# Gated MLP kernel: weight pieces of the second half with raw loads two ahead, at other points of a batch, U and V as one piece

## The chip, the cores and the metric

The kernel runs on one core of a Trainium2 chip. Its time is the device time of one execution in microseconds (us); the median of several executions is compared. The engines are TensorE (PE, with its weight load PEld), VectorE (DVE), ScalarE (ACT) and GpSimd (POOL); SyncE (SP) issues nearly all DMAs. Each engine works through its own instructions in the order in which they are written, and waits for others by semaphores.

## The reference

Three stages follow each other: a linear attention over 8 batches and 8 heads, a gated MLP with a mix over the tokens, and a mix over channels with a low-rank part. Cut to what matters:

```python
# stage 1: attention, 8 batches, 8 heads, 576 tokens, head size 64 -> x (8, 576, 512)
# stage 2
h = np.maximum(x @ w_in, 0.0)                  # w_in 512 x 1024
u, v = h[..., :512], h[..., 512:]
v_n = (v - mean(v)) / sqrt(var(v) + 1e-06)      # over the last axis
v_s = einsum('ts,bsd->btd', w_spatial, v_n) + b_spatial[None, :, None]
x = (u * v_s) @ w_out                          # w_out 512 x 512
# stage 3
u = x + (x.transpose(0, 2, 1) @ U @ V).transpose(0, 2, 1)   # U 576 x 32, V 32 x 576
out = u + np.maximum(u @ w_ch1, 0.0) @ w_ch2   # w_ch1 512 x 2048, w_ch2 2048 x 512
```

The inputs q, k, v and the spatial weights are float32; w_in, w_out, U, V, w_ch1 and w_ch2 arrive as float64, and the kernel turns them into float32 itself.

## The kernel before

A float64 weight comes as pairs of 32-bit words. `fetch_weight` (L35) issues the load of a piece into a tile "raw" (L53) and returns the repack: ACT makes `low` from the low words (L62), DVE makes `bits` in three operations (L67, L71, L75), ACT squares the high words for the size (L80), and a last DVE operation (L87) writes the float32 piece. A full piece is 128 x 512 (512 KB raw). The tiles `low`, `bits` and the stage tile "w32" (`stage`, L170), into which most pieces are written, exist once each; raw loads alternate between "raw" and "raw2" (`raws`, L174). A piece of w_ch1, and half of w_ch2, is written from the stage tile to DRAM (tensors w1d and w2r, 256 KB a piece). Four pairs of w_ch2 rows are repacked into the tile `w2`, POOL makes sums of their blocks in `z2` (`left_sums`), and both are split into a float32r high and low part (`w2s`) and stored (w2d). For the left factors, blocks of w1d are read back and handled likewise (`left`).

Matrix products use such splits: of x = hi + lo three products are summed (hi hi, hi lo, lo hi; `products`, L773). PSUM pool "a" has four banks, which all outputs of the gated stage take in turn, so the tile four places later waits until an output has been read.

The attention runs first, to about 371 us of the span, with its own weight steps for w_in, w_spatial and w_out. Then come eight batches of the gated stage, some 64 us each, and from about 886 us the channel stage. A batch's tokens lie in four tiles of 128 and one of 64. A batch is, in PE's order:

- `gate`: eight outputs pu (four f, two column halves; 12 matmuls of 128 x 288 each), whose relu on ACT (L908) gives u; then eight outputs pz (14 matmuls each) of the normalised values with the spatial weights, which DVE multiplies with u (L929); ACT and POOL (or DVE for the last f) split the result into g.
- `gated_open`, `gated_out`: px, g times w_out, for five token tiles; ACT copies it (L961), DVE splits it (xh, xl).
- `low_rank`: pr, and `low_rank_out` its split t1; `mixed`: transposes pt and py, added on DVE and stored.
- Between these, `values` of the next batch: pv, relu on ACT (L840), for the last tile an addition on DVE (L843) and a maximum (L844); statistics on DVE (L849 to L851), a power on POOL (L852), the normalising (L857) and casts on DVE and the difference on POOL. `normalize` of a tile is called in `values` of the next one, ahead of its statistics.

Weight steps lie between: `work()` (L874) is called four times in the pu loop, twice in the pz loop and twice around the first half of `mixed`. One call does the next step of the piece at hand and, where that ends, issues the load of the piece behind it: so one raw load is under way at a time. Which pieces a batch has is fixed: batch 0 U, V and two of w_ch1, batches 1 to 4 three pieces and a pair of w_ch2 rows each, batch 5 the rest, batches 6 and 7 left factors. A scheduler orders instructions on each engine by the written order and by `issue_after(self.last[...])`, which holds a step's instructions behind the last relu and the last DVE operation noted. ACT sets the whole of `ua` and `ub` to zero with nine copies (L285, L287) before U's parts are written there.

## Time and profile before

| | |
|---|---|
| runs, median (lowest to highest) | 1631.65 us (1629.53 to 1633.07), 3 runs |
| profiled execution, its own time | 1628.22 us |
| its span | 1626.4 us |
| PE busy | 1563.1 us, 96% of the span |
| DVE, ACT, POOL busy | 1170.4, 883.0, 807.8 us (72%, 54%, 50%) |
| mean granted clock of PE | 0.995 |
| attention / gated stage / channel stage | 0 to 371 / 371 to 886 / 886 to 1626 us |

The rows below come from this one execution. A window row gives for a stretch how long each engine was busy, so its length less PE's busy time is PE's idle time there; PEclk is the share of the full clock that PE was granted. A timeline row gives start, length, engine, line and operation, output and inputs, how many instructions were merged, and in brackets the idle time in front of it and the instruction that ended it. In a row of line groups the last part is the idle time before all of them, with what ended most of it.

### The profile page before, as it was taken

What the parts mean: (1) busy time and instruction counts of PE and PEld (TensorE: products, weight loads), DVE (VectorE), ACT (ScalarE), POOL (GpSimd) and SP (SyncE); (2) the same over time, 40 slices, a digit from 0 to 9 for tenths busy, and PEclk for the clock granted to TensorE, in tenths of its full rate; (3) what the DMA queues carried; (4) which work ended last, traced back from release to release, by engine and by line L of the source; (5) the groups of instructions that cost most, each with busy time, mean ns of one, the idle gap of its engine ahead of it and who ended that gap; (6) DMA issues with size and microseconds to landing.
All of it is one profiled execution on the core that took longest, in us unless ns stands there. A gap on an engine that the chain in (4) does not pass through costs nothing.

```text
span 1626.4 us, 30538 instructions
## 1 busy us (share of the span) xinstructions
PE 1563.1 (96%) x11592; PEld 1462.6 (90%) x11592; DVE 1170.4 (72%) x1642; ACT 883.0 (54%) x1668; POOL 807.8 (50%) x610
## 2 busy tenths in 40 slices
PE   7999999998999999999999999999999999999998
PEld 7998889887888888797978899999999999999998
DVE  6888767865766766766565578788877777777765
ACT  5888768883443443443434555555555555555443
POOL 3678777674342443442434256546554455444442
PEclk9999999999999999999999999999999999999999
DMA  4677766652342442533427678999899877777876
GB/s 139 188 204 205 213 189 189 198 146 71 102 136 92 142 130 88 171 98 105 160 96 313 225 242 281 305 315 316 293 343 396 268 231 234 239 248 237 259 242 233
DMA packets 172182, 336.72 MB, mean 207 GB/s; under 512 B 25794, under 2 KB 96610, under 8 KB 168964
## 3 DMA queue, kind: packets, MB, share of 16 engines
q1 hardware_dynamic: 171892, 334.72, 64.1%
q8 instruction: 91, 1.49, 0.4%
q14 instruction: 55, 0.45, 0.1%
q10 hardware_dynamic: 144, 0.07, 0.0%
HBM read 251.58 MB, written 73.55 MB: 200 GB/s over the span
## 4 chain that ended last, share of the span: by engine, by line
PE 69%; DVE 12%; DMA 8%; ACT 5%; issue 3%; POOL 2%; SPq 1%; DVEq 0%; ACTq 0%; POOLq 0%
PE pc L779 19%; PE ph_x L779 11%; PE ph_z L779 6%; PE pv L779 5%; PE pn L616 5%; PE pkv L588 4%; PE pu L779 4%; PE ph_y L779 3%; PE pk L515 2%; PE pt L547 2%; DMA raw_c<-in_w_ch 2%; DMA w1d<-w_c 1%; PE pq L515 1%; PE pt L997 1%; DVE bits_c L67 1%
## 5 line engine op out<-in xcount | busy, mean ns | idle before, releaser
L779 PE MATMUL pc<-hc,w 128*128 128x288 f32 x2688 | 420.3, 295 | 3.2 <-ACT hc L146 1.2
L779 PEld LDWEIGHTS pc<-hc,w 128*128 128x128 f32 x2688 | 378.1, 188 | 4.2 <-ACT hc L146 2.9
L779 PE MATMUL ph_x<-us,cw 128*128 128x288 f32 x1536 | 244.9, 295 | 3.3 <-DVE us L149 3.3
L569 POOL TENSOR_TENSOR qp<-e,qp 128x576 fp32r<-128x576 f32 x128 | 183.9, 1459 | 115.9 <-ACT e L566 87.9
L779 PEld LDWEIGHTS ph_x<-us,cw 128*128 128x128 f32 x1536 | 217.2, 188 | 4.3 <-DVE us L149 3.7
L616 PE MATMUL pn<-qp,kv 128*65 128x288 f32 x768 | 206.0, 328 | 8.8 <-DVE nd L625 4.2
L1096 POOL TENSOR_TENSOR t<-h,h 128x576 f32<-128x576 f32 x64 | 113.4, 1773 | 183.0 <-DVE hc L149 164.7
L149 DVE TENSOR_TENSOR hc<-t,hc 128x576 fp32r<-128x576 f32 x128 | 132.2, 1035 | 50.2 <-ACT hc L146 49.9
L1155 ACT COPY u<-ph_x 128x288 f32<-128x288 f32 x128 | 51.2, 400 | 191.0 <-PE ph_x L779 190.9
L588 PE MATMUL pkv<-v,kp 128*128 128x65 f32 x1024 | 153.1, 252 | 0.0
L588 PEld LDWEIGHTS pkv<-v,kp 128*128 128x128 f32 x1024 | 151.7, 191 | 0.0
L779 PE MATMUL ph_z<-us,cw 128*128 128x288 f32 x768 | 124.5, 297 | 8.7 <-DVE c L1160 8.5
L149 DVE TENSOR_TENSOR hc<-h,hc 128x576 fp32r<-128x576 f32 x96 | 125.0, 1305 | 9.6 <-ACT hc L146 9.5
L779 PEld LDWEIGHTS ph_z<-us,cw 128*128 128x128 f32 x768 | 107.9, 188 | 13.4 <-DVE c L1160 13.1
L1096 POOL TENSOR_TENSOR t<-u 128x576 f32<-128x576 f32 x32 | 48.9, 1528 | 137.6 <-DVE us L149 120.4
L1096 POOL TENSOR_TENSOR t<-h,t 128x576 f32<-128x576 f32 x64 | 111.8, 1748 | 9.0 <-DVE hc L149 6.5
L779 PE MATMUL pz<-wt,vn 128*128 128x288 f32 x768 | 112.5, 295 | 2.3 <-DVE u L929 2.2
L1168 ACT ACTIVATE h<-c 128x288 f32<-128x288 f32 x192 | 85.3, 445 | 54.2 <-DVE c L1160 53.9
L616 PEld LDWEIGHTS pn<-qp,kv 128*65 128x65 f32 x768 | 97.8, 138 | 14.6 <-DVE nd L625 5.4
L779 PE MATMUL pu<-xs,wi 128*128 128x288 f32 x768 | 104.9, 298 | 4.4 <-DVE v L843 4.4
L779 PEld LDWEIGHTS pu<-xs,wi 128*128 128x128 f32 x768 | 104.2, 190 | 5.4 <-DVE v L843 4.6
L779 PEld LDWEIGHTS pz<-wt,vn 128*128 128x128 f32 x768 | 105.2, 188 | 3.1 <-DVE u L929 3.1
(169 smaller groups left out, 3153.3 us busy)
## 6 DMA issues: line engine op xcount, KB each, us to landing
w<-w2d SPq DMA_DIRECT2D x224, 512.0 KB, 4.9
u<-ud SPq DMA_DIRECT2D x16, 1152.0 KB, 5.4
raw_c<-in_w_ch SPq DMA_DIRECT2D x32, 512.0 KB, 4.2
cw<-w1x SPq DMA_DIRECT2D x8, 1792.0 KB, 10.0
v<-in_v SPq DMA_DIRECT2D x32, 325.0 KB, 4.2
k<-in_kT SPq DMA_DIRECT2D x32, 320.0 KB, 3.4
q<-in_qT SPq DMA_DIRECT2D x32, 320.0 KB, 4.0
x<-nd SPq DMA_DIRECT2D x64, 144.0 KB, 3.3
```

The lines of the kernel that those rows point to most:

```text
L67: nc.vector.tensor_scalar(out=bits, in0=hi, scalar1=3, scalar2=0x3FFFFFF8, op0=ALU.logical_shift_left, op1=ALU.bitwise_and,)
L149: return self.put((nc.gpsimd if elo == "pool" else nc.vector).tensor_tensor(out=lo, in0=src, in1=hi, op=ALU.subtract))
L515: self.pin(nc.tensor.matmul(pa[:, j * NF + t, :], x[d, t * P : (t + 1) * P], ws[d, :], start=True, stop=True,))
L547: self.pin(nc.tensor.transpose(pt[:, at, :], s[:, u, :], self.ident))
L569: self.pin(nc.gpsimd.tensor_tensor(out=lo[:, c], in0=e[:, c], in1=hi[:, c], op=ALU.subtract))
L588: self.pin(nc.tensor.matmul(pkv[:, i, j, :], kp[:, j * NF + t, :], vb[:, u * D1 : (u + 1) * D1], start=False, stop=(j == 1 and t == NF - 1),))
L616: self.pin(nc.tensor.matmul(pn, kv[k][:, i, g // 2, :], qp[q][:, i, g * HS : (g + 1) * HS], start=(m == 0), stop=(m == len(terms) - 1),))
L779: self.put(self.nc.tensor.matmul(out, x, y, start=(start and i == 0), stop=(stop and i == len(terms) - 1), skip_group_check=chained,))
L997: nc.tensor.transpose(pt[:, s0 - c0 : s0 - c0 + n], ts[t][0][:n, fs], self.ident[:n, :n])
L1096: self.put(self.nc.gpsimd.tensor_tensor(out=out, in0=p, in1=q, op=ALU.subtract))
L1155: self.put(nc.scalar.copy(out, src))
L1168: self.put(nc.scalar.activation(self.h[n, t // 2, x][:, t % 2], src, AF.Relu))
```

## The change

The late weights (U, V, w_ch1, w_ch2 and the left factors) become one list of 49 units, made once by `units()`. `prefetch()` issues the raw loads of the next two raw units, alternately into "raw" and "raw2"; `work()` does one unit and then prefetches. Each raw unit is a full piece: conversion, last operation and store in one step. U (two copies of its last rows) and V (in two column halves, each held twice) are one piece of 128 x 448 with seven loads and one repack; only the places of `ua` and `ub` that hold no U are zeroed, from a tile of zeros set at the start.

`work()` is now called four times in the pu loop, not in the pz loop, and then once after the px tiles are begun, once behind `low_rank_out` and once in the middle of `mixed`: seven units a batch for batches 0 to 6, none in batch 7. Batches 1 to 3 have store pieces throughout but for the last units of batch 3; pairs, their parts and left factors fill batches 4 to 6. The stage tile, `low` and `bits` still exist once. `low_rank_out` notes its two last instructions in `last`. The pad of `vn` is written behind the values of batch 0 (`pad()`), and a tile's statistics and power are written ahead of the normalising of the tile before it. The order of PE's instructions is the same. New line numbers: L67, L71, L75, L87 become L111, L115, L118, L121; L62 and L80 become L110 and L120; L908 becomes L937; L929 becomes L958.

```diff
+    def fetch(self, parts, name):
+        nc, raw = self.nc, None
+        if any(src.dtype != F32 for _, src in parts):
+            tag, pool = (("raw", self.sp), ("raw2", self.mq))[self.fetched % 2]
+            self.fetched += 1
+            raw = pool.tile([P, 2 * PIECE], I32, tag=tag, name=f"{tag}_{name}", bufs=1)
+            for view, src in parts:
+                nc.sync.dma_start(view(raw, 2), src.bitcast(I32))
+
+        def into(dst):
+            if raw is not None:
+                return repack_doubles(nc, self.sp, dst, raw, name)
...
+        def low_rank():
...
+            into = self.fetch(parts, "uv")
+
+            def step():
+                a = self.stage("uv", c1 + HS)
+                into(a)
...
+                nc.scalar.copy(ub[:, :, 2 * R : 3 * R], z)
+                nc.scalar.copy(ua[tail:, NF, 2 * R : 3 * R], z[tail:, 0])
+                for i in (0, 1, 3):
+                    nc.scalar.copy(ua[:, :, i * R : (i + 1) * R], w)
+                    nc.scalar.copy(ub[:, :, i * R : (i + 1) * R], w[:, :NF])
...
+                for h in range(2):
+                    r, c = slice(h * R, (h + 1) * R), slice(h * HS, (h + 1) * HS)
+                    for i in range(3):
+                        nc.scalar.copy(vs[i * R : (i + 1) * R, c], v[r])
...
         def piece(dst, src, name):
             def load():
+                into = self.fetch([(whole, src)], name)
+
+                def step():
+                    w = self.stage(name, PIECE)
+                    into(w)
                     nc.sync.dma_start(dst, w)
+                return step
             return load
...
+    def prefetch(self):
+        raws = 0
+        for i, u in enumerate(self.todo):
+            kind, f, step = u
...
+            if kind == "raw":
+                raws += 1
+                if raws > 2:
+                    break
+                if step is None:
+                    u[2] = f()
+
+    def work(self):
+        if not self.todo:
+            return
+        kind, f, step = self.todo.pop(0)
+        with self.tc.issue_after(self.last[0]), self.tc.issue_after(self.last[1]):
+            (step if kind else f)()
+        self.prefetch()
...
@@ values
-        self.normalize()
         st = mq.tile([P, 6], F32, tag="st", name=f"st{b}_{t}", bufs=2)
...
         nc.gpsimd.tensor_tensor(
             out=rstd[:n], in0=rstd[:n], in1=self.mhalf[:n, :1], op=ALU.pow
         )
+        self.normalize()
@@ gate
-            if f < self.KH - 2:
-                self.work()
@@ low_rank_out
-        nc.scalar.copy(t1, pr)
+        act = nc.scalar.copy(t1, pr)
...
+        self.last[:2] = act.ins, dve.ins
@@ main loop
+    mx.units()
+    mx.prefetch()
     for t in range(NST):
         mx.values(0, t)
+    mx.pad()
...
         begun = [mx.gated_open(b, t) for t in range(3)]
+        mx.work()
```

DVE in the gate of batch 2, before, where pu ends and pz begins (`bits_c`, `w_c` and `w` belong to weight pieces, `u_0` and `u_1` are multiplied with pz):

```order
L67 TENSOR_SCALAR bits_c_3_512_6231<-raw_c_3_512_6198 128x512
L71 SCALAR_TENSOR_TENSOR bits_c_3_512_6231<-raw_c_3_512_6198,bits_c_3_512_6231 128x512
L929 TENSOR_TENSOR u_0_6082<-pz_0_0_6242,u_0_6082 128x288
L75 ISA bits_c_3_512_6231<-bits_c_3_512_6231,low_c_3_512_6229 128x1024
L929 TENSOR_TENSOR u_0_6082<-pz_0_1_6260,u_0_6082 128x288
L87 SCALAR_TENSOR_TENSOR w_c_3_512_6197<-low_c_3_512_6229,bits_c_3_512_6231 128x512
L67 TENSOR_SCALAR bits_c_1_0_6282<-raw_c_1_0_6239 128x512
L71 SCALAR_TENSOR_TENSOR bits_c_1_0_6282<-raw_c_1_0_6239,bits_c_1_0_6282 128x512
L929 TENSOR_TENSOR u_1_6118<-pz_1_0_6288,u_1_6118 128x288
L75 ISA bits_c_1_0_6282<-bits_c_1_0_6282,low_c_1_0_6280 128x1024
L929 TENSOR_TENSOR u_1_6118<-pz_1_1_6306,u_1_6118 128x288
```


and after:

```order
L111 TENSOR_SCALAR bits_c_3_1536_6223<-raw_c_3_1536_6149 128x512
L115 SCALAR_TENSOR_TENSOR bits_c_3_1536_6223<-raw_c_3_1536_6149,bits_c_3_1536_6223 128x512
L118 ISA bits_c_3_1536_6223<-bits_c_3_1536_6223,low_c_3_1536_6222 128x1024
L958 TENSOR_TENSOR u_0_6106<-pz_0_0_6275,u_0_6106 128x288
L121 SCALAR_TENSOR_TENSOR w_c_3_1536_6221<-low_c_3_1536_6222,bits_c_3_1536_6223 128x512
L111 TENSOR_SCALAR bits_c_4_6264<-raw_c_4_6190 128x512
L115 SCALAR_TENSOR_TENSOR bits_c_4_6264<-raw_c_4_6190,bits_c_4_6264 128x512
L958 TENSOR_TENSOR u_0_6106<-pz_0_1_6293,u_0_6106 128x288
L118 ISA bits_c_4_6264<-bits_c_4_6264,low_c_4_6263 128x1024
L958 TENSOR_TENSOR u_1_6151<-pz_1_0_6311,u_1_6151 128x288
L121 SCALAR_TENSOR_TENSOR w_c_4_6262<-low_c_4_6263,bits_c_4_6264 128x512
L958 TENSOR_TENSOR u_1_6151<-pz_1_1_6329,u_1_6151 128x288
```


The first multiplication by u_0 stood ahead of two operations of the third piece and stands now ahead of the last one alone; the second has moved from ahead of that piece's last operation (L87, now L121) to behind it and behind two operations of a fourth store piece. The second multiplication by u_1 stood ahead of a last operation into `w2` and stands now behind one into the stage tile.

ACT in the gate of batch 0, before (L908 is the relu of pu; `low_u` is a part of U being repacked, `ub` a copy of U):

```order
L908 ACTIVATE u_1_4777<-pu_1_1_4792 128x288
L62 ACTIVATE low_u_4806<-raw_u_4775 128x128
L80 ACTIVATE low_u_4806<-raw_u_4775 128x128
L908 ACTIVATE u_2_4818<-pu_2_0_4819 128x288
L908 ACTIVATE u_2_4818<-pu_2_1_4833 128x288
L62 ACTIVATE low_u_4847<-raw_u_4814 64x32
```


and after (L937 is the relu):

```order
L120 ACTIVATE low_uv<-raw_uv 128x448
L937 ACTIVATE u_1_4804<-pu_1_1_4819 128x288
L353 CAST ua<-w_uv 128x5x32
L354 CAST ub<-w_uv 128x4x32
L353 CAST ua<-w_uv 128x5x32
L354 CAST ub<-w_uv 128x4x32
L353 CAST ua<-w_uv 128x5x32
L354 CAST ub<-w_uv 128x4x32
L362 CAST vs<-w_uv 32x288 x6
L110 ACTIVATE low_c_0_0_4834<-raw_c_0_0_4611 128x512
L937 ACTIVATE u_2_4845<-pu_2_0_4846 128x288
```


The relu of the third u, first half, stood behind one small piece of U; it stands now behind the whole of U and V, six copies to `ua` and `ub`, six to `vs`, and the first conversion of a piece of w_ch1.

DVE at the first values tile of batch 0, before (`w_pad` is the pad, `st_0`, `mv_0` and `rstd_0` the statistics):

```order
L849 BN_STATS st_0_4624<-v_0_4607 128x6
L648 RECIPROCAL den_31_4569<-den_31_4569 128x9
L765 MEMSET w_pad 64x512
L850 BN_AGGR mv_0_4625<-st_0_4624 128x2
L767 MEMSET w_pad 1x512 x2
L851 TENSOR_SCALAR rstd_0_4626<-mv_0_4625 128x1
L768 CAST vn_4600<-w_pad 64x512
L857 TENSOR_SCALAR v_0_4607<-v_0_4607,mv_0_4625,rstd_0_4626 128x512
```


and after:

```order
L807 MEMSET w_pad 64x512
L809 MEMSET w_pad 1x512 x2
L640 TENSOR_TENSOR kv_31_4471<-pkv_4391,kv_31_4470 128x260
L663 TENSOR_SCALAR nd_4483<-pn_1_4492,eps 65x288
L686 RECIPROCAL den_29_4465<-den_29_4465 128x9
L663 TENSOR_SCALAR nd_4533<-pn_1_4542,eps 65x288
L686 RECIPROCAL den_30_4526<-den_30_4526 128x9
L810 CAST vn_4602<-w_pad 64x512
L890 BN_STATS st_0_4631<-v_0_4614 128x6
L686 RECIPROCAL den_31_4571<-den_31_4571 128x9
L891 BN_AGGR mv_0_4632<-st_0_4631 128x2
L892 TENSOR_SCALAR rstd_0_4633<-mv_0_4632 128x1
```


The pad's memsets stood among the statistics of the first tile; they stand now in front of the last attention operations, and the cast of the pad ahead of the first statistics.

## Rows read from the trace of the kernel before

**Rows 1.** Windows by batch: from:to length, busy us PE, PEld, DVE, ACT, POOL; PEclk.

```profile
370.96:434.29 63.33, 56.70 (x329) 50.99 (x328) 40.46 (x84) 27.32 (x69) 25.46 (x23) 0.97 0.32 99
434.29:497.70 63.41, 61.05 (x359) 53.04 (x358) 43.92 (x81) 27.35 (x56) 23.80 (x24) 1.00 0.38 121
497.70:559.97 62.27, 60.61 (x359) 53.20 (x358) 45.38 (x82) 27.41 (x56) 24.81 (x24) 1.00 0.40 123
559.97:623.67 63.70, 61.23 (x358) 53.04 (x358) 43.63 (x82) 27.39 (x56) 23.81 (x24) 1.00 0.39 120
623.67:688.28 64.61, 61.13 (x359) 53.11 (x358) 47.39 (x82) 27.31 (x56) 28.48 (x28) 1.00 0.41 127
688.28:755.19 66.91, 63.62 (x358) 54.91 (x358) 44.42 (x85) 27.26 (x56) 20.48 (x20) 0.95 0.34 99
755.19:820.25 65.06, 61.30 (x359) 53.16 (x358) 43.28 (x76) 27.04 (x55) 29.37 (x28) 1.00 0.43 141
820.25:886.50 66.25, 65.55 (x384) 57.58 (x384) 38.32 (x74) 25.42 (x51) 24.22 (x24) 0.98 0.55 214
```

**Rows 2.** Windows, as rows 1, of four short stretches with PE stalls.

```profile
393.00:396.50 3.50, 3.34 (x14) 3.34 (x15) 2.64 (x6) 0.05 (x1) 1.41 (x2) 0.51 0.11 44
418.00:421.00 3.00, 2.93 (x19) 2.75 (x20) 2.62 (x6) 2.43 (x6) 1.82 (x2) 1.00 0.28 62
748.10:754.90 6.80, 5.91 (x14) 4.24 (x15) 5.71 (x11) 3.23 (x7) 0.00 (x0) 0.50 0.41 116
819.80:823.20 3.40, 3.40 (x9) 2.63 (x9) 2.27 (x5) 0.00 (x0) 0.00 (x0) 0.51 0.00 0
```

**Rows 3.** Timeline of PE: start, length, instructions [idle before <-released by].

```profile
393.16 9.69 PE L779 MATMUL pu<-xs,wi 128*128 128x288 f32 x60 [4.41 <-DVE v L843]
...
418.07 1.85 PE L779 MATMUL pz<-wt,vn 128*128 128x288 f32 x12 [2.21 <-DVE u L929]
...
749.00 3.78 PE L791 MATMUL px<-wo,gt 128*128 128x512 f32 x8 [3.00 <-ACT x L961]
```

**Rows 4.** Timeline of ACT, batch 5.

```profile
745.72 0.67 ACT L62 ACTIVATE low_c<-raw_c 128x512 int32<-128x512 uint32 x1 [2.56 <-DMA raw_c<-in_w_ch]
```

**Rows 5.** Line groups of DVE, 434:755: count | busy, mean ns | idle, releasers.

```profile
L67 DVE TENSOR_SCALAR bits_c<-raw_c 128x512 int32<-128x512 int32 x27 | 27.0, 1001 | 17.2 <-DMA raw_c<-in_w_ch 16.6
L71 DVE SCALAR_TENSOR_TENSOR bits_c<-raw_c,bits_c 128x512 int32<-128x512 int32 x27 | 22.5, 835 | 0.8
L75 DVE CUSTOM_DVE_ANT_0 bits_c<-bits_c,low_c 128x1024 uint16<-128x1024 uint16 x27 | 21.7, 804 | 2.7 <-ACT low_c L62 1.2
L87 DVE SCALAR_TENSOR_TENSOR w_c<-low_c,bits_c 128x512 f32<-128x512 f32 x18 | 17.5, 971 | 20.0 <-DMA w1d<-w_c 12.3 <-ACT low_c L80 7.8
```

**Rows 6.** Timeline of ACT, gate of batch 0.

```profile
382.49 0.30 ACT L285 CAST ua<-w_z 128x128 fp32r<-128x128 f32 x1 [5.23 <-DVE rstd L851]
...
404.37 0.78 ACT L311 CAST ua<-w_u 128x160 fp32r<-128x160 f32 x3 [0.25 <-DVE w_u L87]
...
415.19 2.05 ACT L337 CAST vs<-w_v 32x576 fp32r<-32x576 f32 x3 [0.83 <-DVE w_v L87]
```

**Rows 7.** Timeline of DVE, first operation on U.

```profile
397.23 1.30 DVE L67 TENSOR_SCALAR bits_u<-raw_u 128x128 int32<-128x128 int32 x1
```

**Rows 8.** Timeline of DVE, gate of batch 2.

```profile
520.65 1.51 DVE L67 TENSOR_SCALAR bits_c<-raw_c 128x512 int32<-128x512 int32 x1
...
524.77 0.69 DVE L87 SCALAR_TENSOR_TENSOR w_c<-low_c,bits_c 128x512 f32<-128x512 f32 x1 [0.89 <-ACT low_c L80]
...
529.97 1.66 DVE L87 SCALAR_TENSOR_TENSOR w_c<-low_c,bits_c 128x512 f32<-128x512 f32 x1 [2.49 <-DMA w1d<-w_c]
```

**Rows 9.** Timeline of PE, gate of batch 2.

```profile
515.61 12.90 PE L779 MATMUL pu<-xs,wi 128*128 128x288 f32 x96
528.35 1.76 PE L779 MATMUL pz<-wt,vn 128*128 128x288 f32 x12
```

More of the change, by code (lines that the diff above doesn't have):

```diff
@@ L98, in fetch_weight, with repack_doubles @@
     return repack
+def repack_doubles(nc, pool, dst, raw, name):
+    n = dst.shape[1]
+    pair = raw[:, : 2 * n].rearrange("p (c two) -> p c two", two=2)
+    lo, hi = pair[:, :, 0], pair[:, :, 1]
+    low, bits = (
+        pool.tile([P, PIECE], I32, tag=t, name=f"{t}_{name}", bufs=1)[:, :n] for t in ("low", "bits")
+    )
+    nc.scalar.activation(low, lo.bitcast(U32), AF.Copy, scale=2.0**-29)
+    nc.vector.tensor_scalar(
+        out=bits, in0=hi, scalar1=3, scalar2=0x3FFFFFF8,
+        op0=ALU.logical_shift_left, op1=ALU.bitwise_and,
+    )
+    nc.vector.scalar_tensor_tensor(
+        out=bits, in0=hi, scalar=-0x40000000, in1=bits, op0=ALU.bitwise_and, op1=ALU.bitwise_or
+    )
+    nc.vector.tensor_tensor(out=bits, in0=bits, in1=low, op=ALU.add)
+    size = low.bitcast(F32)
+    nc.scalar.activation(size, hi.bitcast(F32), AF.Square)
+    nc.vector.scalar_tensor_tensor(
+        out=dst, in0=size, scalar=TINY * TINY, in1=bits.bitcast(F32), op0=ALU.is_ge, op1=ALU.mult
+    )
 class Mixer:
@@ L160, in alloc_weights @@
         nc.vector.memset(self.mhalf, -0.5)
+        self.zero = wp.tile([P, self.NF, self.R], F32, name="zero")
+        nc.vector.memset(self.zero, 0.0)
         self.wo = [wp.tile([P, self.KH, self.DM], F32R, name=f"wo{i}") for i in range(2)]
@@ L419, in pair @@
-            return load
-        def left(m):
-            def load():
-                w = self.mq.tile([P, 4, self.DM // 2], F32, tag="w2", name=f"w1_{m}", bufs=1)
-                self.raw_blocks(w, 1, m)
-                return lambda: sums(w)
-            def sums(w):
-                z = self.mq.tile([P, 4, self.DM // 2], F32, tag="z2", name=f"z1_{m}", bufs=1)
-                self.left_sums([w[:, x] for x in range(4)], z)
-                return part(w, z, 0)
-            def part(w, z, k):
-                n, src = (4, z) if k else (3, w[:, :3])
-                d = self.mq.tile([P, 2, 4, self.DM // 2], F32R, tag="w2s", name=f"w1s_{m}_{k}", bufs=1)
+                into = self.fetch([(whole, self.w_ch2[r, :])], f"c2_{m}_{i}")
@@ new lines, in step @@
+                def step():
+                    if i == 0:
+                        w.append(self.mq.tile([P, 2, self.DM], F32, tag="w2", name=f"w2_{m}", bufs=1))
+                    into(w[0][:, i])
+                    if i:
+                        z.append(self.mq.tile([P, 4, HALF], F32, tag="z2", name=f"z2_{m}", bufs=1))
+                        self.left_sums(
+                            [w[0][:, i, j * HALF : (j + 1) * HALF] for i, j in ((0, 0), (1, 0), (1, 1), (0, 1))],
+                            z[0],
+                        )
@@ new lines, in pair, with left, step, part @@
+            return [("raw", lambda: load(0)), ("raw", lambda: load(1)), (None, part(0)), (None, part(1))]
+        def left(m):
+            w, z = [], []
+            def load():
+                w.append(self.mq.tile([P, 4, HALF], F32, tag="w2", name=f"w1_{m}", bufs=1))
+                self.raw_blocks(w[0], 1, m)
+                def step():
+                    z.append(self.mq.tile([P, 4, HALF], F32, tag="z2", name=f"z1_{m}", bufs=1))
+                    self.left_sums([w[0][:, x] for x in range(4)], z[0])
+                    part(0)
+                return step
+            def part(k):
+                n, src = (4, z[0]) if k else (3, w[0][:, :3])
+                d = self.mq.tile([P, 2, 4, HALF], F32R, tag="w2s", name=f"w1s_{m}_{k}", bufs=1)
@@ L872, in normalize, with gate @@
             f()
-    def work(self):
-        rest, jobs = self.rest, self.jobs
-        if rest:
-            with self.tc.issue_after(self.last[0]), self.tc.issue_after(self.last[1]):
-                f = rest.pop()()
-            if f:
-                rest.append(f)
-        if jobs and not rest:
-            rest.append(jobs.pop(0)())
-    def gate(self, b, jobs):
+    def gate(self, b):
         nc, mq, xs = self.nc, self.mq, self.xs
@@ L1471, in favor_gmlp_mixer_kernel @@
         mx.work()
-        assert not mx.jobs and not mx.rest
         mx.mixed(b, ts, t1, range(KD // 2, KD))
```

213 lines of the change are left out of this document (83 added, 130 removed).

## Prediction

> **What bounds the kernel now.** I read first the stretches, one for each of the eight batches of the gated stage [rows 1]. By the sums of the eight rows TensorE (PE) is busy 491.2 of 515.5 us, VectorE (DVE) 346.8, ScalarE (ACT) 216.5 and GpSimd (POOL) 200.4: PE sets the pace, and what the others do counts only where PE waits for it. By stretch less busy, PE waits 6.6, 2.4, 1.7, 2.5, 3.5, 3.3, 3.8 and 0.7 us in batches 0 to 7, 24.3 in all. To that comes the clock. In stretches of 3.5, 6.8 and 3.4 us PE was granted 0.50 to 0.51 of full speed (1.2 GHz of 2.4) [rows 2], each at a stall or right behind a row of them; half of each stretch is lost, 1.7 + 3.4 + 1.7 = 6.8 us. So some 31 us is all that the edited stage can give back.
>
> Then I looked at the longest waits on PE's timeline: 4.41 us in batch 0's gate, for the last tile of values on DVE, and 3.00 us before the last px of batch 5, for an ACT copy [rows 3]; that copy stood behind an ACT row that had waited 2.56 us for a raw load [rows 4]. Last the line groups of DVE over batches 1 to 5: before its 27 first operations of a piece (L67) DVE was idle 17.2 us, 16.6 of it for raw loads, and before 18 final ones (L87) 20.0 us, 12.3 of it for the store of w_c [rows 5]. The change takes one of these two waits away and leaves the other.
>
> **Raw loads two pieces ahead, from two buffers.** This removes the 16.6 us of DVE's waits and ACT's of the same kind. On PE's path they are worth only what PE lost by them. In batch 5 that is the 3.00 us and the half clock behind it (3.4); in batch 6 about a third of its 3.8, and the 1.7 of clock that follows; in batch 4 about half of its 3.5, since the pieces there go through the tile w2 and not through the single stage tile. Late next is POOL's chain (the differences of x, of the gate's output and of the sums), whose order in a batch stays as it was. For it I leave waits of 1.7 in batch 4, 3.1 in batch 5, 2.6 in batch 6 and 0.4 in batch 7. The gains are then 1.8, 0.2 + 3.4, 1.2 + 1.7 and 0.3, together 8.6 us. Bounds: 2.1, if POOL's chain alone made the waits of batches 5 and 6 and they stay; 16.4, if all of batches 4 to 7 goes (11.3 idle, 5.1 clock).
>
> **Batch 0: what goes.** ACT's nine zero copies, at which ACT stood 5.23 us with the values' relus queued behind [rows 6], and the pad memsets among DVE's statistics. Without these the last values tile reaches DVE 3 to 4 us earlier, and of the 4.41 us about 1 stays. The statistics ahead of the normalising bring nothing more here: by the changed order DVE still normalises a tile of batch 0 before the next tile's statistics.
>
> **Batch 0: what comes.** U and V are one step, and ACT has its sixteen instructions ahead of the relu of the fifth pu (u_2, first half). The repack began at 397.23, when the values were done [rows 7]; 3 to 4 us earlier that is 394, and low words, bits and size take about 2.5 behind it. Then come six copies to ua and ub at 0.26 (0.78 for three [rows 6]), 1.6 in all, and six of V's halves with 288 columns each; of those one costs between half of 0.68 and all of it (2.05 for three copies of 576 columns, same rows), 2.0 to 4.1 together, and I take 2.4, near the half, as the work halves. With the next piece's first conversion (0.7) the relu is at about 401.2. The first pz needs its bank at 393.16 - 4.41 + 60 x 0.133 + 1 = 397.7 (60 of the 96 pu matmuls were left [rows 3]): a wait of 3.5 us. With 1 in front and 0.7 elsewhere batch 0 waits 5.2 us (3.0 to 7.5), and with an even chance it falls to half clock for a stretch, 0.9 on average. Gain 6.6 + 1.7 - 5.2 - 0.9 = 2.2 us, bounds -0.9 and 5.3.
>
> **Batches 1 to 3: what it costs.** Before, two pieces end ahead of DVE's first multiplication by u, and the others lie across pz and the mixed part; now four in a row begin in pu, and two of them reach into pz. Each goes through the one stage tile, so its final operation (now L121) waits until the store of the piece before has landed. The trace has this once: a final operation began at 524.77 and took 0.69, the next began at 529.97, 4.5 us behind the first one's end, with DVE idle for 2.49 of it [rows 8]. A piece then comes every 4.5 + 0.7 to 1.7 = 5.2 to 6.2 us. By DVE's work alone (1.00 + 0.84 + 0.80 + 0.97 [rows 5]) it would be 3.6.
>
> Let P be the gate's first pu matmul (515.61 in batch 2). The 96 of pu take 12.74, so one takes 0.133 and the 14 of a pz 1.86 [rows 9], and the sixth pz would start at P + 12.74 + 5 x 1.86 = P + 22.0. It takes the bank of the second pz and needs the second multiplication by u_0 (now L958), which DVE has behind the third piece's final operation and two operations of the fourth piece. Before, the gate's first piece began on DVE at P + 5.0 (520.65 [rows 8]). Now two whole pieces, 7.2 us of DVE, lie among the next batch's values, where idle time takes up half of them: I take P + 8.5. The first final operation is then done at P + 12.7, the second at P + 18, the third begins at P + 22.5 and is done at P + 23.3 to 24.1; two more operations and the multiplication end near P + 25. That is a wait of 3.0 us. Ahead of it the fourth pz needs the last relu, which ACT has behind the third piece's first conversion, and so behind the second final operation: 1.0 (0 to 1.7). With 0.3 elsewhere each of these batches waits 4.3 us, 12.9 in place of 2.4 + 1.7 + 2.5 = 6.6: a loss of 6.3 us. Bounds: 0.7 each, a gain of 4.5 (no final operation waits); 6.5 each and half clock (1.7) behind each, a loss of 18.
>
> On the store's price the Trainium skill, "DMA: Bandwidth & Descriptors", section "Anatomy of one DMA — SWDGE (gpsimd) path", gives about 2.0 us fixed plus bytes by 436 GB/s, for 256 KB an estimate of 2.6 us; by it no final operation would wait, and the sum would be the first rival's. The 4.5 us of [rows 8] speaks against it (these stores are issued by SP), and the measurement decides.
>
> **The rest.** The seven U and V loads and the raw loads stand on SP's queue ahead of their use; a late one would cost what raw loads cost now, and the range has that. The pad memsets lie beside the attention's last outputs, and nothing needs them before batch 0's pz; without that cover they cost 0.5 to 1.5 once. The mixed part's t1 now holds back the weight step behind it, but DVE had that order already.
>
> **Sum.** 8.6 + 2.2 - 6.3 = 4.5 us less. The profiled execution took 1628.22 (span 1626.4), and the runs' median 1631.65 lies 3.4 above it. The difference is taken from the median: 1627.2.
>
> **Rivals.**
> First, the stores are hidden: the pieces' own 3.6 us and idle ACT time cover most of the landing. For it: 7.8 of the 20.0 us before final operations were ACT's [rows 5], and the store bit about once a gate. Against: then only two store pieces stood close together, now four do. Batches 1 to 3 would wait 0.7 each: 8.6 + 2.2 + 4.5 = 15.3 less, 1616.3.
>
> Second, the other side: the single stage tile makes the gates of batches 1 to 3 worse than that. From the third final operation beginning at P + 24 each us later is one of PE, three times over, and a wait of 3 us brings half clock as at 749.00 [rows 2, 3]. At 6.5 + 1.7 a batch that is a loss of 18; with 8.6 and 1.3 back elsewhere 8 us slower, 1639.7. For it: two final operations took 0.69 and 1.66 [rows 8], so a piece can be a whole us longer. Against: the wait of 2.21 at 418.07 left the clock at 1.00 [rows 2, 3].
>
> The Trainium skill, "SBUF — State Buffer", section "SBUF: two separate sides", has DVE and POOL lock a shared port for a whole instruction. By that rule every final operation beside POOL's xs would wait for its end, which would move this case towards the second rival; the 1.66 against 0.69 of [rows 8] agrees with it.
>
> Third, the waits only change place, from raw loads to stores and to ACT's U and V block, and cancel within 3 us: 1629 to 1634. For it: the sum is small against its parts.
>
> **How the numbers follow.** Forecast 0.38, first rival 0.21, second 0.24, third 0.17. A measurement of this kernel tells about 0.2%, 3.3 us, from no change: faster means under 1628.4. That is 0.30 of the forecast's 0.38 and the first rival, 0.51; the same is 0.08 of it and the third, 0.25; slower 0.24. The range that leaves out 2 in 10 goes from 1614 to 1640, the forecast's own from 1622 to 1631.
>
> **What would show it.** Right: no DVE or ACT wait of over 1 us for raw_c in batches 1 to 6; the 4.41 in batch 0's pu down to about 1, and some 3 us at its first pz for ACT's relu; in batches 1 to 3 waits at the fourth and the sixth pz (1 and 3 us), with DVE idle for the store of w_c ahead of them; no 3.00 before the last px of batch 5. Wrong: no waits in those pz (first rival), or half clock behind them (second); px and pr of batches 4 to 6 waiting as before, which would mean that raw loads did not hold them.

## The result, and the profile after

The changed kernel takes 1616.63 us (median of 4 runs, 1614.21 to 1619.34) beside 1631.95 for the kernel before (4 runs, 1629.53 to 1633.07). The ratio is 0.9909, 95% interval 0.9889 to 0.9928: 15 us faster, three times the 4.5 that were forecast, inside the range. The profiled execution took 1617.40 us, its span is 1615.6.

The windows by batch of the changed kernel answer to [rows 1] (columns as there; each begins at the batch's first pv):

```profile
376.12:437.27 61.15, 56.61 (x329) 50.90 (x327) 38.28 (x72) 26.84 (x61) 26.01 (x23) 0.97 0.41 126
437.27:499.81 62.54, 60.60 (x359) 53.39 (x357) 45.90 (x87) 27.81 (x57) 22.03 (x20) 1.00 0.41 127
499.81:562.41 62.60, 60.61 (x359) 53.39 (x357) 45.88 (x87) 27.77 (x57) 22.04 (x20) 1.00 0.42 127
562.41:625.29 62.88, 60.85 (x358) 53.43 (x357) 46.09 (x87) 27.89 (x57) 22.64 (x21) 1.00 0.39 122
625.29:686.08 60.79, 60.07 (x359) 53.32 (x358) 38.81 (x77) 26.58 (x55) 28.08 (x27) 1.00 0.40 126
686.08:747.93 61.85, 60.53 (x359) 53.17 (x357) 41.57 (x80) 26.94 (x56) 29.16 (x28) 1.00 0.36 107
747.93:807.73 59.80, 59.80 (x359) 53.28 (x357) 35.89 (x66) 25.81 (x50) 35.69 (x36) 1.00 0.49 166
807.73:872.26 64.53, 63.84 (x383) 56.25 (x381) 35.70 (x72) 23.70 (x49) 21.46 (x20) 1.00 0.45 179
```

Stretch less PE's busy time is now 4.5, 1.9, 2.0, 2.0, 0.7, 1.3, 0.0 and 0.7 us: 13.2 in all, where [rows 1] had 24.3. The last window ends at the matmul that stood at 886.02 before, so the gated stage went from 515.1 us (370.96 to 886.02) to 496.1, 18.9 less: batch 0 2.0 less, batches 1 to 3 1.4 less (189.4 to 188.0), batches 4 to 7 15.5 less (262.5 to 247.0); the batches of before are cut at their first pv here too, 0.16 us ahead of the cuts of [rows 1] at 434.29 and 623.67.

That is more than the spans differ (10.8), because the profiled execution lost time elsewhere, where nothing was edited. One stretch of the attention by the clock of the trace, in the changed kernel and then before:

```profile
236.00:245.50 9.50, 7.12 (x47) 6.79 (x47) 3.67 (x5) 3.17 (x4) 6.58 (x5) 0.69 0.62 182
```

```profile
236.00:245.50 9.50, 8.48 (x82) 8.04 (x82) 6.69 (x8) 5.66 (x8) 5.73 (x5) 1.00 0.67 179
```

The granted clock is 0.69 in one and 1.00 in the other, with 47 matmuls in 9.5 us and not 82. At the same place of the program PE had waited 2.38 us for DVE (to 239.99) in the changed kernel and 1.59 us (to 237.02) before; from the pk in front of it to the next pq it took 11.3 us (236.03 to 247.30) and 7.5 us (233.85 to 241.33). Such stretches come and go between executions: the second profile of the changed kernel has none there, and the gated stage begins at 370.96 in the profile of before and at 373.8 to 380.2 in the thirteen others of this study, one of which has this part unedited (375.3, the kernel before with another choice of buffers). The length of the gated stage in the trace therefore tells kernels apart better than an execution's time; two profiles of one kernel differ by 0.9 and 2.0 us in it.

Of the 2.0 us between the two profiles of the changed kernel 1.5 are batch 0 (61.2 and 59.7 us). PE waits 3.46 and 3.47 us there for the first pz, and behind it the granted clock is 0.57 in one profile and 1.00 in the other:

```profile
406.68:410.68 4.00, 4.00 (x18) 4.00 (x19) 3.16 (x4) 3.13 (x7) 1.91 (x2) 0.57 0.43 107
```

```profile
405.25:409.25 4.00, 4.00 (x30) 4.00 (x31) 3.17 (x4) 3.10 (x7) 1.91 (x2) 1.00 0.40 105
```

The waits of PE that are left, on its timeline (they answer to [rows 3]):

```profile
401.36 1.86 PE L821 MATMUL pu<-xs,wi 128*128 128x288 f32 x12 [1.08 <-ACT u L937]
406.68 3.11 PE L821 MATMUL pz<-wt,vn 128*128 128x288 f32 x12 [3.46 <-ACT u L937]
...
479.67 1.85 PE L821 MATMUL pz<-wt,vn 128*128 128x288 f32 x12 [1.31 <-DVE u L958]
...
518.58 12.89 PE L821 MATMUL pu<-xs,wi 128*128 128x288 f32 x96
...
542.25 1.85 PE L821 MATMUL pz<-wt,vn 128*128 128x288 f32 x12 [1.49 <-DVE u L958]
...
604.56 1.85 PE L821 MATMUL pz<-wt,vn 128*128 128x288 f32 x12 [1.45 <-DVE u L958]
```

The 4.41 us for the last values tile are gone. Batch 0 waits 1.08 and 3.46 us for ACT's relus, batches 1 to 3 wait 1.3 to 1.5 us once each at the sixth pz (in batch 2 at 542.25, its pu having begun at 518.58), and the 3.00 us before the last px of batch 5 are gone too. DVE's line groups over batches 1 to 5 answer to [rows 5] (L111 was L67, L121 was L87):

```profile
L111 DVE TENSOR_SCALAR bits_c<-raw_c 128x512 int32<-128x512 int32 x28 | 20.4, 730 | 0.4
L121 DVE SCALAR_TENSOR_TENSOR w_c<-low_c,bits_c 128x512 f32<-128x512 f32 x20 | 17.6, 881 | 14.1 <-ACT low_c L120 5.6 <-DMA w1d<-w_c 5.1 <-DMA w2r<-w_c 3.4
```

The idle time for raw_c went from 16.6 us to nothing that the row names (0.4 in all). For stores it is 5.1 + 3.4 where 12.3 stood.

### The profile page after: what moved, and what is told of

Its sections match the earlier page's. It is cut to its first block, busy times and chain, and to the rows that moved or that the text cites. A ratio compares the mean times of both kernels' runs of the same rounds, so it can differ in the third digit from the quotient of the medians.

```text
span 1615.6 us, 30512 instructions
## 1 busy us (share of the span) xinstructions
PE 1564.5 (97%) x11592; PEld 1470.8 (91%) x11592; DVE 1153.1 (71%) x1627; ACT 880.2 (54%) x1656; POOL 813.9 (50%) x610
## 4 chain that ended last, share of the span: by engine, by line
PE 73%; DVE 9%; DMA 7%; issue 3%; POOL 3%; ACT 3%; SPq 1%; DVEq 0%; ACTq 0%; POOLq 0%
PE pc L821 19%; PE ph_x L821 11%; PE ph_z L821 6%; PE px L821 5%; PE pn L654 4%; PE pv L821 4%; PE pkv L626 4%; PE pz L821 4%; PE ph_y L821 3%; PE pu L821 2%; PE pk L553 2%; PE pt L585 1%; PE pq L553 1%; DVE hc L174 1%; POOL qp L607 1%
```

## The experiments

The table has the gated stage of each profile, from batch 0's first pv to the ph_x matmul of batch 7 that stands at 886.02 in the kernel before; from here on this length is compared first, and the times with their ratios to the kernel before stand beside it.

| kernel | time, us | ratio (95%) | gated stage, us |
|---|---|---|---|
| before | 1631.95 | | 370.96 to 886.02: 515.1 |
| changed | 1616.63 | 0.9909 (0.9889 to 0.9928) | 376.12 to 872.26: 496.1 |
| changed, again | 1616.15 | 0.9870 (0.9847 to 0.9893) | 374.62 to 868.68: 494.1 |
| loads one ahead | 1615.74 | 0.9904 (0.9882 to 0.9927) | 374.76 to 870.03: 495.3 |
| two steps in pz | 1619.57 | 0.9926 (0.9907 to 0.9944) | 375.34 to 876.92: 501.6 |
| one raw buffer | 1622.50 | 0.9909 (0.9892 to 0.9927) | 377.52 to 878.04: 500.5 |
| one raw buffer, steps in pz | 1644.65 | 1.0052 (1.0034 to 1.0069) | 376.17 to 897.19: 521.0 |
| before, buffers in turn | 1626.44 | 0.9938 (0.9915 to 0.9961) | 375.27 to 880.02: 504.8 |
| normalising first | 1615.39 | 0.9873 (0.9853 to 0.9893) | 374.46 to 869.25: 494.8 |
| stage and w2 in turn | 1614.28 | 0.9896 (0.9879 to 0.9913) | 373.75 to 869.18: 495.4 |
| store first | 1619.73 | 0.9885 (0.9848 to 0.9923) | 379.69 to 877.53: 497.8 |
| U and V early | 1620.54 | 0.9928 (0.9910 to 0.9945) | 378.43 to 874.30: 495.9 |
| three edits | 1611.90 | 0.9850 (0.9828 to 0.9872) | 380.21 to 869.93: 489.7 |
| three edits, again | 1611.77 | 0.9851 (0.9826 to 0.9877) | 378.56 to 867.41: 488.8 |

The kernel before took 1631 us on the chips of the first runs and 1636 on the others, so times of different groups are compared by ratio.

**Loads one ahead.**

```diff
-                if raws > 2:
+                if raws > 1:
```

> The changed kernel with the raw loads one unit ahead in place of two; places and pieces as changed. Theory A (the raw loads were what held batches 4 to 6): DVE again waits for raw_c, over 8 us in all over batches 1 to 5 (0.4 in the changed kernel, 17.2 before), and the time is 4 to 9 us above the changed kernel's 1616.6, so 1621 to 1626. Theory B (where the steps stand did it, none in pz): DVE's waits come back in part, but PE does not see them; within 2 us of 1616.6.

The gated stage took 495.3 us, and DVE's wait for raw_c did not come back:

```profile
L111 DVE TENSOR_SCALAR bits_c<-raw_c 128x512 int32<-128x512 int32 x28 | 20.4, 730 | 0.4
```

Theory A is refuted: the depth of the loads is worth nothing here. But the waits did not come back either, so theory B's ground was wrong as well. A load that is issued when the unit ahead of it is done was what the kernel before had too, and there DVE waited 16.6 us. What differs is which buffer the load goes to.

**Two steps in pz.**

```diff
+            if f < self.KH - 2:      # in the pz loop
+                self.work()
...
         begun = [mx.gated_open(b, t) for t in range(3)]
-        mx.work()
...
         ahead(1)
-        mx.work()
         mx.mixed(b, ts, t1, range(KD // 2))
```

> The changed kernel with two of a batch's seven weight steps in the pz loop (behind its first two f), in place of the one behind the begun px and the one behind low_rank_out; loads two ahead as changed. Theory A: within 3 us of 1616.6, since the loads are there in time wherever a step stands. Theory B: waits of px for DVE's multiplications of u and of px for ACT's copies come back in batches 1 to 6, 1 to 2 us a batch; 1623 to 1630.

The stage grew by 5.5 us, with the loads in time (0.5 us of DVE idle before L111). PE's waits in the gated stage:

```profile
PE pz L821 <- DVE u L958: 5.6, 6, 1.4
...
PE px L821 <- POOL g L174: 2.2, 3, 0.9
PE px L821 <- DVE u L958: 2.1, 3, 1.2
```

The waits for DVE's multiplications and POOL's differences are 9.9 us here; in the changed kernel the first two come to 4.6 and 1.3 and the third is not listed. So where the steps stand is worth some 5 us in the trace: 3.6 in batches 0 to 3 and 2.5 in batch 5, while batches 4, 6 and 7 are as short as in the changed kernel (60.2, 59.8 and 64.5 us). The time alone, 2.9 us above 1616.6, lies just within what theory A allowed.

**One raw buffer.** On top of loads one ahead:

```diff
-            tag, pool = (("raw", self.sp), ("raw2", self.mq))[self.fetched % 2]
+            tag, pool = "raw", self.sp
```

> The changed kernel with loads one unit ahead and all raw units in the one buffer raw, so that a load waits until ACT has read the piece before (in batch 5 of the kernel before, all pieces had one buffer). Steps where the change put them. Theory C (a load that waits for its buffer is the wait for raw_c, and PE loses by it wherever the steps stand): DVE waits for raw_c 2 to 4 us a piece again, and the gated stage takes 502 to 512 us by the trace (496.1 in the changed kernel, 495.3 with two buffers and loads one ahead, 515.1 before). Theory D (such waits cost PE only where steps stand in pz): the same DVE waits, but the gated stage within 3 us of 496.

**One raw buffer, steps in pz.** Both edits.

> One raw buffer and loads one ahead as in the kernel above, and two of the seven steps in the pz loop, as in the run with steps in pz (501.6 us gated stage). Theory C: the one above's loss and the pz loop's 5.5 add up, 507 to 518 us. Theory D: only here do raw waits meet DVE's multiplications of u; over 508 us while the run above stays at 496 to 499. If neither buffers nor loads matter to PE at all: 501 to 503 us.

DVE waited 34.7 and 48.1 us for raw_c in the two. First the kernel without steps in pz, then the one with them:

```profile
L111 DVE TENSOR_SCALAR bits_c<-raw_c 128x512 int32<-128x512 int32 x28 | 21.4, 764 | 34.7 <-DMA raw_c<-in_w_ch 34.7
```

```profile
L111 DVE TENSOR_SCALAR bits_c<-raw_c 128x512 int32<-128x512 int32 x27 | 16.0, 593 | 48.1 <-DMA raw_c<-in_w_ch 48.1
```

PE lost 4.4 us in the first (against 496.1; 5.2 against loads one ahead with two buffers) and 19.4 more than the two-buffer kernel in the second (521.0 against 501.6), nearly all of it in batches 0 to 3. What the raw waits meet in pz shows in PE's waits of the second:

```profile
PE px L833 <- ACT x L990: 14.1, 5, 4.4
```

Four of the five are the last px of batches 0 to 3 (2.44, 4.39, 3.68 and 3.02 us); the fifth, 0.60 us in batch 7, is in nearly every kernel here. In batch 1 ACT's copies stand behind a conversion that waited for its raw load. ACT, then PE:

```profile
504.92 0.67 ACT L110 ACTIVATE low_c<-raw_c 128x512 int32<-128x512 uint32 x1 [4.59 <-DMA raw_c<-in_w_ch]
505.50 1.56 ACT L990 COPY x<-px 128x512 f32<-128x512 f32 x3
```

```profile
506.13 3.16 PE L833 MATMUL px<-wo,gt 128*128 128x512 f32 x8 [4.39 <-ACT x L990]
```

It is the same picture as [rows 3, 4], and half clock comes with it (mean granted clock 0.95 to 0.98 in these four batches). In the kernel without steps in pz no px waits for ACT's copies but the one in batch 7. Both theories were half right: a shared buffer cost 4 to 5 us with the steps outside pz (theory C's kind, below its range) and four times that with two of them in pz (theory D's kind).

**The kernel before, with its buffers in turn.** As written, a piece of w_ch2 gets its buffer by `raws(len(jobs))`, and `jobs += [row(m), row(m + self.NM)]` asks for two pieces while the list has the same, even length. So all w_ch2 pieces of batches 5 and 6 that go through the stage tile (five of the seven pieces of batch 5) had the one buffer "raw"; that the buffers alternate, as the text ahead of the prediction has it, was true only among the pieces of w_ch1 and within a pair. A pair begins with "raw", and in batches 1 and 3 the piece ahead of it had "raw" too. The waits for raw_c stand just there: 3.0, 4.0, 9.6 and 3.7 us in batches 1, 3, 5 and 6 of the kernel before, none over 0.1 in batches 2 and 4. In batch 3 it is the first piece of the pair:

```profile
603.00 0.43 DVE L67 TENSOR_SCALAR bits_c<-raw_c 128x512 int32<-128x512 int32 x1 [4.02 <-DMA raw_c<-in_w_ch]
```

```diff
     def raws(self, i):
-        return ("raw2", self.mq) if i % 2 else None
+        self.fetched = getattr(self, "fetched", 0) + 1
+        return ("raw2", self.mq) if self.fetched % 2 else None
...
         def piece(dst, src, name):
-            raws = self.raws(len(jobs))
             def load():
                 w = self.stage(name, PIECE)
-                repack = fetch_weight(nc, self.sp, w, src, name, raws=raws)
+                repack = fetch_weight(nc, self.sp, w, src, name, raws=self.raws(0))
```

> The kernel before with one edit: raw loads of the late weights take the two buffers strictly in turn. (As written, the buffer goes by the length of the job list, and both rows of a w_ch2 pair of pieces got the same one, so in batch 5 all pieces shared one buffer.) If the shared buffer is what made the waits for raw_c there, DVE's 16.6 us over batches 1 to 5 fall by 6 us or more, batch 5 loses its 3.0 us wait at px and the half clock, and the gated stage takes 507 to 512 us in place of 515.1. If issuing the load only when a step is done is the cause, the waits stay and the stage is within 2 us of 515.

The stage is 504.8 us, 10.3 less than before, by this edit alone and below the 507 to 512 that were expected, and DVE's idle time before L67 is 0.7 us in all:

```profile
L67 DVE TENSOR_SCALAR bits_c<-raw_c 128x512 int32<-128x512 int32 x27 | 28.1, 1040 | 0.7
```

By batch it is 2.0 us in batch 0, 1.3, 0.0 and 1.4 in batches 1 to 3, 0.2 lost in batch 4, and 2.8, 1.5 and 1.5 in batches 5 to 7: outside batches 0 and 7, the gain is where the waits were. Batch 5 went from 66.9 to 64.1 and no px waits 3 us any more. What PE still waits for in the stage is DVE (its multiplications by u, the last values tile of batch 0, the splits xl):

```profile
PE px L778 <- DVE u L928: 7.6, 5, 1.6
PE pu L778 <- DVE v L842: 3.9, 1, 3.9
PE pr L976 <- DVE xl L149: 3.0, 2, 1.5
```

So about half of the gain is the buffer: 10.3 of the 18.9 us by the traces, 9.4 of 19.7 by the times on one chip (1635.86 before, 1626.44, 1616.15). The remaining 8.7 come from all other edits together. Of these the place of the steps was tested (some 5 us, above), but not on this kernel, and the new order of the pieces was not run by itself.

**Normalising first.**

```diff
             nc.vector.tensor_scalar_max(v[:n], v[:n], 0.0)
+        self.normalize()
...
             out=rstd[:n], in0=rstd[:n], in1=self.mhalf[:n, :1], op=ALU.pow
         )
-        self.normalize()
```

> The changed kernel with the normalising of a tile ahead of the next tile's statistics again, as before; nothing else. If the order of statistics and normalising is worth nothing (as the prediction has it for batch 0), each batch's time in the trace stays within 0.5 us and the gated stage within 2 us of 496.1. If it is part of the gain, the first piece of a gate starts later behind its first pu matmul (6.9 us in batch 2 of the changed kernel) and batches 1 to 3 lose 1 us or more each.

The stage took 494.8 us, batches 1 to 3 186.4 (188.0 and 187.0 in the two profiles of the changed kernel). The order of statistics and normalising is worth nothing that these runs can tell.

**Stage tile and w2 in turn.**

```diff
                 def step():
-                    w = self.stage(name, PIECE)
+                    self.pieces = getattr(self, "pieces", 0) + 1
+                    if self.pieces % 2:
+                        w = self.stage(name, PIECE)
+                    else:
+                        w = self.mq.tile([P, 2, self.DM], F32, tag="w2", ...)[:, 0]
                     into(w)
                     nc.sync.dma_start(dst, w)
```

> The changed kernel with every second store piece written into the tile w2 in place of the one stage tile, so that a last operation need not wait for the store of the piece just before. If the waits of pz at 479.67, 542.25 and 604.56 (1.3, 1.5, 1.45 us) are the store's, they go and the time falls by 3 to 5 us: 1612 to 1614. If they come from the order alone (the second multiplication of u_0 stands behind the fourth piece's operations and DVE is busy until then), they stay at over 1 us and the time is within 1.5 us of 1616.6.

All waits of the last operation for a store are gone, and those at the sixth pz are 0.80, 0.87 and 0.47 us:

```profile
L121 DVE SCALAR_TENSOR_TENSOR w_c<-low_c,bits_c 128x512 f32<-128x512 f32 x20 | 17.4, 869 | 9.2 <-ACT low_c L120 9.2
```

```profile
477.20 1.85 PE L825 MATMUL pz<-wt,vn 128*128 128x288 f32 x12 [0.80 <-DVE u L962]
...
538.91 1.84 PE L825 MATMUL pz<-wt,vn 128*128 128x288 f32 x12 [0.87 <-DVE u L962]
...
600.12 1.84 PE L825 MATMUL pz<-wt,vn 128*128 128x288 f32 x12 [0.47 <-DVE u L962]
```

Batches 1 to 3 fall from 188.0 to 184.6 us, as expected. The time did not clearly follow (0.9896 beside 0.9909): batch 5 took 63.9 us against 61.9, with a wait for POOL of 1.26 at a px and half clock behind it (mean granted clock 0.97 in that batch, 1.00 in the changed kernel's). Some half of the pz waits is the store's; the rest, which stays without it, is DVE's order.

**Store first.**

```diff
-                    nc.sync.dma_start(dst, w)
+                    self.stored = nc.sync.dma_start(dst, w).ins
...
-        self.prefetch()
+        if self.stored is None:
+            self.prefetch()
+        else:
+            with self.tc.issue_after(self.stored):
+                self.prefetch()
```

> The changed kernel with each piece's store issued ahead of the next raw load, not 0.7 us behind it as in the changed kernel's SP order. If a store lands late (4.5 us from the end of its last operation in batch 2's gate) because 512 KB of raw load were issued just ahead of it, the waits of the last operations for w1d and w2r (8.5 us over batches 1 to 5) fall to under 3 us, and the pz waits of 1.3 to 1.5 us in batches 1 to 3 to under 1. If the landing is the store's own time, both stay as they are, or the loads behind it come later and DVE waits for raw_c over 2 us in all.

The median from issue to landing falls to 2.4 and 2.8 us (4.4 and 4.1 over the same batches of the changed kernel), and no last operation waits for a store:

```profile
w1d<-w_c SPq DMA_DIRECT2D x12, 256.0 KB, 2.4
...
w2r<-w_c SPq DMA_DIRECT2D x8, 256.0 KB, 2.8
```

The expectation on the landing holds, but the stage did not get shorter (497.8, of which some 1.6 are half clock in batch 5): DVE waits 3.0 us for raw_c, and now the stores of the outputs (ud) are issued right behind a raw load and land 4.0 and 3.6 us (medians) behind their issue, where 2.6 and 2.4 stood in the changed kernel. ACT's copy into the next output tile waits for them, 4.31 us here where 1.50 stood, and pu for its bank (4.0 us in three waits):

```profile
522.74 0.43 ACT L1037 COPY uo<-pt 128x320 f32<-128x320 f32 x1 [4.31 <-DMA ud<-uo]
```

The lateness goes to what is issued behind the load.

The 4.5 us of [rows 8] are thus not the store's own. In the kernel before that store, too, was issued 0.7 us behind a raw load:

```profile
524.77 0.33 SPq L53 DMA_DIRECT2D raw_c<-in_w_ch  x1
525.49 0.32 SPq L359 DMA_DIRECT2D w1d<-w_c  x1
```

On SP's timeline of the changed kernel a raw load is issued 0.7 us ahead of the first store (529.94) and 2.6 us ahead of the second (535.22):

```profile
529.21 0.33 SPq L311 DMA_DIRECT2D raw_c<-in_w_ch  x1
529.94 0.32 SPq L377 DMA_DIRECT2D w1d<-w_c  x1
532.66 0.33 SPq L311 DMA_DIRECT2D raw_c<-in_w_ch  x1
535.22 0.32 SPq L377 DMA_DIRECT2D w1d<-w_c  x1
```

On DVE the last operation after the first store waited, the next one did not:

```profile
525.43 1.50 DVE L111 TENSOR_SCALAR bits_c<-raw_c 128x512 int32<-128x512 int32 x1
...
529.22 0.69 DVE L121 SCALAR_TENSOR_TENSOR w_c<-low_c,bits_c 128x512 f32<-128x512 f32 x1 [0.74 <-ACT low_c L120]
...
534.50 0.69 DVE L121 SCALAR_TENSOR_TENSOR w_c<-low_c,bits_c 128x512 f32<-128x512 f32 x1 [2.57 <-DMA w1d<-w_c]
...
537.96 1.10 DVE L121 SCALAR_TENSOR_TENSOR w_c<-low_c,bits_c 128x512 f32<-128x512 f32 x1 [0.38 <-ACT low_c L120]
```

The Trainium skill, "DMA: Bandwidth & Descriptors", section "Anatomy of one DMA — SWDGE (gpsimd) path", gave the estimate of 2.6 us for these 256 KB; the section is on DMAs issued by POOL, and these are issued by SP. The 2.4 and 2.8 of the rows above agree; the 4.5 that I took as deciding against it is a store behind 512 KB of load.

**U and V early.** Besides the line shown, `work()` passes over the notes in `last` that are still empty.

```diff
     mx.pad()
+    mx.work()
     for b in range(B):
         mx.gate(b)
```

> The changed kernel with the unit of U and V done during the values of batch 0, ahead of its gate, the gate's four steps being pieces of w_ch1. If the 1.08 and 3.46 us that batch 0 waits for ACT's relus, and the half clock behind the second (1.7), are due to the block of U and V copies, both waits go and the time falls by 3 to 6 us: 1611 to 1614. If ACT is late for another reason, or if the values' relus wait behind the block in turn, it is within 1.5 us of 1616.6.

The ACT wait at the first pz and the half clock went, but batch 0 is no shorter than the changed kernel's two profiles leave open (60.7 beside 61.2 and 59.7): its gate now has four store pieces, and PE waits for DVE and once for ACT. The time, 1620.54, fits neither side of the expectation, while the stage is as long as the changed kernel's.

```profile
397.51 6.61 PE L824 MATMUL pu<-xs,wi 128*128 128x288 f32 x48 [1.27 <-DVE v L888]
405.67 1.59 PE L824 MATMUL pu<-xs,wi 128*128 128x288 f32 x10 [1.55 <-ACT u L940]
...
419.35 1.86 PE L824 MATMUL pz<-wt,vn 128*128 128x288 f32 x12 [1.48 <-DVE u L961]
```

**Three edits.** Stage and w2 in turn, U and V early, and no step behind batch 0's first pu:

```diff
             us.append(u)
-            self.work()
+            if b or f:
+                self.work()
```

> Three edits on the changed kernel: every second store piece through the tile w2, the U and V unit during the values of batch 0, and no weight step behind the first pu of batch 0's gate. If the gains add up (3.5 us in batches 1 to 3 from the first; from the others batch 0's two ACT waits of 1.1 and 3.5 us and its half clock, less the 2.8 us of DVE waits that U and V early with four store pieces in that gate left), the gated stage takes 487 to 491 us (496.1 in the changed kernel) and the time is 1608 to 1613. If the waits only move on to DVE in batch 0, 492 to 494 us and 1612 to 1615.

The stage took 489.7 us; batch 0 57.2 (61.2 and 59.7 changed). PE's idle time in it is 7.8 us by the window of 380.21 to 869.93. Stage and time are within what was expected if the gains add up.

> The changed kernel as it is, beside the kernel of three edits on the same chip: 1613 to 1620, gated stage 494 to 498 us; the spread between executions shows how much the clock in the attention and the channel stage moves the time.

> The kernel of three edits again, on the same chip as the changed kernel: 4 to 8 us below it, gated stage 488 to 492 us. If its first result was chance, within 2 us of it.

Side by side the changed kernel took 1616.15 (494.1 us gated stage) and the three edits 1611.77 (488.8): 4.4 us less, at the low end of the expectation. The intervals of the two ratios, 0.9847 to 0.9893 and 0.9826 to 0.9877, overlap; the trace's 5.3 us, against a spread of 1 to 2 between profiles of one kernel, is clearer.

## Why the prediction was right and wrong

The direction and the range were right, and the forecast's sum was a third of what came. By its steps:

- **Batch 0**: 2.2 us forecast, 2.0 measured (3.5 in the second profile), and each piece of it: about 1 us left of the 4.41 (1.08, though now for ACT's relu and not for DVE), a wait of 3.5 at the first pz behind the U and V block (3.46), and half clock behind it (in the trace 0.62 granted from 406.5 to 411). The half clock had an even chance in the forecast and is a matter of chance: it did not come in the second profile, and that is the difference. That the sum fits is luck in part, for the kernel before with its buffers in turn takes 61.2 us there as well, without these edits. ACT's rows show the block, 2.66 us for the six V copies where 2.4 were taken:

```profile
400.40 0.60 ACT L120 ACTIVATE low_uv<-raw_uv 128x448 f32<-128x448 f32 x1 [5.99 <-DVE bits_uv L118]
...
402.98 2.66 ACT L362 CAST vs<-w_uv 32x288 fp32r<-32x288 f32 x6
...
406.23 1.00 ACT L937 ACTIVATE u<-pu 128x288 f32<-128x288 f32 x3
```

- **Batches 1 to 3**: a loss of 6.3 forecast, a gain of 1.4 measured. The step that failed is the price of a piece, "every 4.5 + 0.7 to 1.7 = 5.2 to 6.2 us": one store that landed behind a raw load was taken for every store. The first piece behind it was late, as forecast (2.57 us of waiting), the next was 3.5 us later. The start of the chain was mis-sized too: 6.9 us behind the first pu (525.43 less 518.58) and not 8.5. The third piece's last operation so began at P + 19.4 (537.96), not P + 22.5, and the wait at the sixth pz was 1.3 to 1.5, not 3.0. The wait of 1.0 at the fourth pz did not come at all. And the sum had nothing for raw loads in batches 1 to 3, where the buffer is worth 2.8 us (batches 1 and 3); beside the kernel before with its buffers in turn (186.6) the changed kernel is 1.4 and 0.4 us longer in its two profiles. The store's waits cost 3.4 and 2.4 us there, as stage tile and w2 in turn shows (184.6 against 188.0 and 187.0).
- **Batches 4 to 7**: 8.6 forecast, 15.5 measured. By the kernel before with its buffers in turn, 5.5 of these are the raw loads': 2.8 in batch 5 and 3.0 in batches 6 and 7 (3.6 and 3.2 forecast), and nothing in batch 4, where 1.8 were forecast though DVE waited 0.1 us for its raw loads there. The other 10.0 are the step that failed, "For it I leave waits of 1.7 in batch 4, 3.1 in batch 5, 2.6 in batch 6": POOL's chain was taken as late next because its order did not change, and no row had shown it as the last to end. With the buffers in turn the waits of PE over 0.5 us that are left in batches 4 to 6 are for DVE (1.60 and 1.50 in batch 4, 1.21 in batch 5, 1.50 in batch 6) and ACT (1.18 in batch 5), none for POOL; in the changed kernel these are gone, PE's idle time is 0.7, 1.3 and 0.0, and POOL is named for the 1.3 of batch 5 alone. The upper bound of 16.4 in that part was the right end. Whether the steps' places or the other pieces in these batches took DVE's waits away is open: two steps back in pz brought none of it back in batches 4 and 6.
- **The mechanism**: that late raw loads reach PE through ACT's copies was right, and the kernel before with its buffers in turn shows it for batches 5 and 6 (the 3.00 us ahead of the last px become 1.18, the 1.90 of batch 6 go). That it was the loads' distance, "two pieces ahead", was wrong: with one ahead the stage is as short. It was a buffer that two pieces shared, which I had in [rows 4] as a wait and did not follow to the tile.
- **The rivals**: the first rival's time (1616.3) is the measured one, but by another way, and that is luck: the gated stage gained 18.9 us in the trace and not its 15.3, and the executions show 15 us of it (the profiled one lost time in the attention). Its condition, that stores are hidden in batches 1 to 3, holds only in part; its sum lacked the 6.9 us more in batches 4 to 7. The second rival's point, a last operation later than P + 24, was not reached. On the third, that the waits only change place: batch 0 is such a case.

Batch 5 takes 59.8 us where U and V came early, and 61 to 64 elsewhere. In the early kernel every later step stands one place ahead, and its batch 6 takes 64.7 us, with a wait of 2.17 us for POOL's difference of g. Where the steps stand as in the changed kernel, batch 5 has such waits (0.4 to 2.0 us) and takes 61.5 to 62.1 us at a granted clock of 1.00, or 63.7 to 63.9 at 0.97.

What stays open: how the 8.7 us beside the buffer divide among the other edits; and how much of each kernel's time in the attention and the channel stage is chance. The zero copies and the pad were not tested by themselves. The kernel before has one profile only.

## What to carry to other kernels

When a load waits, ask which tile it lands in before asking how far ahead it is issued: follow the wait to the buffer and to its last reader. A wait on an engine beside the bound costs what stands behind it in that engine's order, so the same kind of wait cost 4 to 5 us in one place and 19 in another. The landing time of one transfer belongs to its place in the queue: look at what was issued just ahead of it before taking it for every transfer of its kind. And test a chain that is "late next" on a row that shows it ending last.

## What the runs showed of the hardware

A 256 KB store to DRAM landed 2.4 to 2.8 us behind its issue (medians) when it was issued ahead of a 512 KB load, and 4.1 to 4.4 us in the order of the changed kernel, where the one that landed late in batch 2 stood 0.7 us behind a load. The output stores of 160 and 128 KB went from 2.6 and 2.4 us to 4.0 and 3.6 when they came right behind a load in turn.

A stall of PE need not have the same end in every execution. Eight profiles have the wait of 3.46 or 3.47 us at the first pz of batch 0; in seven of them PE ran at half clock behind it, and in one, of the same kernel as another of the seven, at 1.00, which is worth 1.5 us. In the attention, whose matmuls are the same in number and shape before and after, one stretch ran at 0.69 of the clock behind a wait of 2.38 us, and at 1.00 behind a wait of 1.59 us in another profile: 11.3 us and 7.5 us for the same work. That alone moves the time of an execution by as much as several of the edits here.
